# Four of the third batch's six head pairs transposed by DMA instead of by TensorE

## The chip, the cores and the metric

The kernel runs on one core of a Trainium2 chip. The metric is the device time of one execution in microseconds (us). The engines are called as in the profile: PE (TensorE matmul) and PEld (its weight load), DVE (VectorE), ACT (ScalarE), POOL (GpSimd) and SP (SyncE, which here only issues DMAs). Batches are counted from 0 as in the code: the "third batch" is batch 2.

## The reference

Attention with a squared ReLU in place of the softmax, followed by a gated feed-forward network whose gate is a ReLU. There are 8 batches, 12 heads, 448 positions and 64 elements per head; the network goes from 768 to 1536 and back to 768.

```python
scores = scale * np.matmul(q, k.transpose(0, 1, 3, 2))
attn = np.maximum(scores, 0.0) ** 2 / S
attn_out = np.matmul(attn, v)
x = attn_out.transpose(0, 2, 1, 3).reshape(B * S, H * D)
gate = np.maximum(x @ w_gate, 0.0)
val = x @ w_val
out = (gate * val) @ w_out
```

## The kernel before

The twelve heads of a batch are worked as six pairs, two pairs to a "quad". `k`, `q` and `v` of a batch are loaded by POOL's DMA queue in their natural layout and cast to bf16 on the way (`load_qk`, `load_v`, line 95), into two sets of buffers `kn`, `qn`, `vn` that alternate by batch. The scores need `k` and `q` with the head's 64 elements on the partitions, so both have to be transposed. There are two ways in the kernel:

- By PE, for batches 0 to 2 (`transposes`, lines 177 and 179): sixteen transposes of a pair go into one PSUM tile `kq_ps`, eight from `kn` and eight from `qn`, and one DVE copy brings them to `kq_sb`. `kq_ps` shares its three PSUM buffers with the score tiles `sc_ps`.
- By DMA, for batches 3 to 7 (`dma_transposes`, lines 151 and 154): DVE regroups `kn` into `kr` and `qn` into `qr`, one copy each for all twelve heads, and SP issues eight DMA transposes, four that write `kT` and four that write `qT`. `kr` and `qr` exist once, `kT` and `qT` twice (`NB` is 2). For batch b+1 this is done in the third of the eight steps of batch b.

The order of the work on every engine is the program's order: each instruction is pinned. `batch(b)` runs eight steps. A step n issues three tiles (`burst`: score tiles, or the begun product of a quad with `v`), squares the first two, and fills two gaps with units of the feed-forward network of batch b-1 (`gap`, `gv_unit`, `out_unit`). Work in `midway` is run in the middle of the next such unit; the PE transposes are put there by this table:

```python
PAIRS_AT = {0: [2], 1: [3], 3: [4], 4: [5], 7: [6, 7]}
```

Pairs 6 and 7 stand for pairs 0 and 1 of the next batch. `operands` returns the transposed tiles of a pair, and where `b >= PE_B` it only points at `kT` and `qT` and issues nothing. So batch 2's pairs 0 and 1 are transposed at the end of batch 1, its pairs 2 and 3 in steps 0 and 1 of batch 2, and its pairs 4 and 5 in steps 3 and 4. The first score tile of pair 2 is the last of the three tiles of step 2.

In the last step (n is 7) the product with `v` of the third quad is finished by `values()`, whose DVE cast (line 458) writes `xT`. SP also issues the stores of the output tiles `o_sb` (line 302), two for each tile of 128 rows, from three buffers. An output tile is scaled by ACT (line 294) before.

`load_qk(b + 1)` and `load_v(b + 1)` stand in step 0 of batch b, but POOL does little else and runs ahead in its queue until the buffer that a load writes is free.

Of the kernel before, what the change touches and what calls it, by code (L numbers as in the profile page):

```python
# [16 lines left out]
def kernel(  # L17
# [15 lines left out]
    nc = tc.nc  # L33

    B, H, S, D = q.shape
    d_model, d_ff = moe_w_gate.shape
# [3 lines left out]
    HP = H // 2  # L40
# [19 lines left out]
    def pin(ins):  # L60
        return tc.keep_in_program_order(ins)
# [53 lines left out]
    def load_qk(b, h0=0, h1=H):  # L115
        load_nat(kn_b[b % NB], k, b, h0, h1)
        load_nat(qn_b[b % NB], q, b, h0, h1)

    def load_v(b):
        load_nat(v_b[b % NB], v, b, 0, H)  # L120

    def low_values(b):

        t = v_b[b % NB].rearrange("p (q s h) i d -> p q s h i d", s=2, h=2)
        pin(nc.vector.tensor_copy(t[64:128, :, 1, :, 3, :], t[0:64, :, 1, :, 3, :]))
# [14 lines left out]
            dma_in(wo_sb[c], rows.rearrange("(kf p) m -> p kf m", p=128))  # L140


    PE_B = 3
    kT_b = [const.tile([128, HP, 512], BF16, name=f"kT{i}") for i in range(NB)]
    qT_b = [const.tile([128, HP, 512], BF16, name=f"qT{i}") for i in range(NB)]
    def dma_transposes(b):

        n = b % NB
        for nat, grp, tr in ((kn_b[n], kr, kT_b[n]), (qn_b[n], qr, qT_b[n])):
            o = grp.rearrange("p i (h d) -> p i h d", d=D)  # L150
            pin(nc.vector.tensor_copy(o, nat.rearrange("p h i d -> p i h d")))
            for i in range(4):
                r = 128 if i < 3 else 64
                pin(nc.sync.dma_start_transpose(out=tr[:, :, i * 128:i * 128 + r], in_=grp[0:r, i, :]))


    def operands(b, hp, bank=None):

        if b >= PE_B:
            n = b % NB  # L160
            return kT_b[n][:, hp, 0:S], qT_b[n][:, hp, 0:S]
        kq = transposes(b, hp, bank)
        return kq[:, 0:S], kq[:, 512:512 + S]
# [4 lines left out]
    def transposes(b, hp, bank):  # L168
        if bank is None:
            ps = psum.tile([128, 2048], BF16, name="kq_ps", tag="sc", bufs=3)  # L170
        else:
            ps = bank.bitcast(BF16)
        for t, c0 in ((kn_b[b % NB], 0), (qn_b[b % NB], 512)):
            for i in range(4):
                for h2 in range(2):
                    o = ps[h2 * 64:h2 * 64 + 64, c0 + i * 128:c0 + i * 128 + 128]
                    pin(nc.tensor.transpose(o, t[:, 2 * hp + h2, i, :], ident))  # L177
        kq = kqpool.tile([128, 512 + S], BF16, name="kq_sb")
        pin(nc.vector.tensor_copy(kq, ps[:, 0:512 + S]))
        return kq  # L180
# [9 lines left out]
    def relu2(src, dst, n):  # L190
        square_part(dst, relu_part(src, n))
# [25 lines left out]
    def av_rest(b, qd, attn, banks):  # L217
        for c in range(2):
            for i in range(3):
                for h2, o in HALVES:  # L220
                    mm(banks[c][o, :], v_b[b % NB][:, 4 * qd + 2 * c + h2, i, :], attn[:, 8 * c + 2 * i + h2, :], False, i == 2)
# [100 lines left out]
    def start_gaps(of):  # L322
        share[:] = [len(ffn), of, 0]

    def gap():

        n, of, i = share
        for _ in range((i + 1) * n // of - i * n // of):
            ffn.pop(0)()
        flush()  # L330
        share[2] = i + 1
# [22 lines left out]
    def transpose_pair(b, hp, bank=None):  # L354
        kqs[b, hp] = operands(b, hp, bank)

    def attn_of(b, qd):
        if (b, qd) not in attns:
            attns[b, qd] = atpool.tile([128, 14, S], BF16, name="attn")
        return attns[b, qd]  # L360

    def burst(b, tiles):

        todo, begun = [], None
        for qd, kind, c, i in tiles:
            attn = attn_of(b, qd)
            if kind == "pair":
                todo.append(scores(kqs[b, 2 * qd + c], i, attn, 8 * c + 2 * i))
            elif kind == "last":
                todo.append(scores_last((kqs[b, 2 * qd], kqs[b, 2 * qd + 1]), attn))  # L370
            else:
                ps = sc_tile()
                banks = [ps[:, c, :S] for c in range(2)]
                av_last(b, qd, attn, banks)
                begun = (qd, banks, ps[:, :, :S])
        return todo, begun
# [59 lines left out]
    def batch(b):  # L436

        gaps = [(1, 1)] * 8
        if b == 1:
            gaps = [(0, 1), (0, 1), (0, 1), (0, 1), (0, 1), (0, 1), (1, 1), (1, 1)]  # L440
        elif b == 2:
            gaps[5] = (0, 2)
        start_gaps(sum(map(sum, gaps)))
        for n in range(len(tiles_later) // 3):
            todo, begun = burst(b, tiles_later[3 * n:3 * n + 3])
            relu2(*todo[0])
            relu2(*todo[1])
            late.extend(todo[2:])
            if n == 1:
                low_values(b)  # L450
            if n == 0 and b < B - 1:
                load_qk(b + 1)
                load_v(b + 1)

            def values():
                qd, banks, both = begun
                av_rest(b, qd, attn_of(b, qd), banks)
                pin(nc.vector.tensor_copy(xT_of[b][:, 2 * qd:2 * qd + 2, :], both))  # L458

            for _ in range(gaps[n][0]):  # L460
                gap()
            for hp in PAIRS_AT.get(n, ()):
                if hp < HP:
                    midway.append(lambda hp=hp: transpose_pair(b, hp))
                elif b + 1 < B:
                    midway.append(lambda hp=hp: transpose_pair(b + 1, hp - HP))
            if begun and (b, n) == (1, 2):
                midway.append(values)
            elif begun:
                values()  # L470
            if b + 1 < B and n == 2 and b + 1 >= PE_B:
                dma_transposes(b + 1)
            for _ in range(gaps[n][1]):
                gap()

    for b in range(B):
        xT_of[b] = xpool.tile([128, KD, S], BF16, name="xT")
        if b == 0:
            first_batch()
        else:  # L480
            batch(b)
        if b + 1 < B:
            ffn.extend(ffn_units(b))
            if b == 0:
                for _ in range(7):
                    ffn.pop(0)()
                for hp in range(2):
                    midway.append(lambda hp=hp: transpose_pair(1, hp))
                ffn.pop(0)()
# [34 lines left out]
```

## Time and profile before

| | |
|---|---|
| median of 3 runs | 435.25 us (434.73 to 435.25) |
| the profiled execution | 435.1 us, of which the profile's span is 433.3 us |
| granted TensorE clock | 1.00 |
| PE / PEld busy | 98% / 58% of the span |
| DVE / ACT / POOL busy | 49% / 50% / 11% of the span |
| PE transposes of batches 1 and 2 | 192, each row 219 ns |
| `kq_sb` copies on DVE from `kq_ps` | 12, mean 654 ns |
| regrouping copies on DVE | 10, mean 950 and 953 ns |
| DMA transposes | 40, median 2.5 to 2.6 us from issue to landing |

The timeline of an engine shows for each piece its start, its length, the operation with its tiles, how many instructions are merged in it, and in brackets the idle time before it with what ended it. PE matmuls are pipelined: the length of a row holds the drain of the last one, so the pace is read from the starts of rows that follow each other.

### The profile page before, as it was taken

The numbers are of one execution on the slowest core, as the hardware profiler recorded it, in microseconds if no ns is written. First come the engines' busy times: TensorE is split into PE (matmuls) and PEld (weight loads), VectorE is DVE, ScalarE is ACT, GpSimd is POOL, SyncE is SP. The second block draws the span as 40 slices with busy tenths as digits, with TensorE's granted clock in tenths as the row PEclk, the third lists the DMA queues.
The fourth block names the chain that finished last, engine by engine and source line by source line (L and its number), as shares of the span: only waits on it lengthen the run. The fifth ranks groups of instructions, "written<-read, shape, count | busy, mean of one in ns | idle before, by whom it ended". The sixth has DMA issues, their size and how long they took to land.

```text
span 433.3 us, 11436 instructions
## 1 busy us (share of the span) xinstructions
PE 425.4 (98%) x5068; PEld 250.3 (58%) x5068; DVE 210.7 (49%) x334; ACT 218.0 (50%) x325; POOL 49.0 (11%) x71
## 2 busy tenths in 40 slices
PE   8899999999999999999999999999999999999996
PEld 4457655655565555655566555655566555566564
DVE  5952784556623655356532565435643454422210
ACT  4942666454554564465454645554545645532221
POOL 8424311100204000300004000010000000000001
PEclk9999999999999999999999999999999999999999
DMA  9999999905679770591517932170414100030014
GB/s 151 181 205 195 203 205 211 204 5 81 106 145 166 103 112 19 104 198 34 97 38 128 176 66 65 38 138 2 101 29 106 42 2 2 12 100 2 2 38 109
DMA packets 78513, 42.45 MB, mean 98 GB/s; under 512 B 48352, under 2 KB 74976, under 8 KB 78464
## 3 DMA queue, kind: packets, MB, share of 16 engines
q0 software_dynamic: 45120, 23.47, 40.6%
q1 hardware_dynamic: 32992, 18.01, 17.8%
q8 instruction: 39, 0.64, 0.6%
q10 hardware_dynamic: 352, 0.25, 0.2%
q14 instruction: 10, 0.08, 0.1%
HBM read 47.19 MB, written 11.01 MB: 134 GB/s over the span
## 4 chain that ended last, share of the span: by engine, by line
PE 84%; DMA 12%; POOL 2%; issue 1%; POOLq 0%; ACT 0%
PE o_ps L64 25%; PE g_ps L64 23%; PE v_ps L64 22%; PE sc_ps L64 13%; DMA qn<-in_q_dram 5%; DMA wo<-in_moe_w_out_dram 5%; DMA vn<-in_v_dram 2%; POOL qn L95 1%; PE kq_ps L177 1%; POOL kn L95 1%; POOL vn L95 0%; POOL out_dram L302 0%; POOLq L519 0%; ACT o_sb L294 0%; POOL ident L91 0%
## 5 line engine op out<-in xcount | busy, mean ns | idle before, releaser
L184 ACT ACTIVATE r_sb<-sc_ps 128x896 bf16<-128x896 f32 x168 | 145.1, 927 | 39.4 <-PE sc_ps L64 39.4
L188 DVE TENSOR_TENSOR attn<-r_sb 128x896 bf16<-128x896 bf16 x168 | 103.7, 623 | 92.2 <-ACT r_sb L184 92.1
L64 PE MATMUL g_ps<-xT,wg 128*64 128x448 bf16 x1152 | 126.1, 354 | 0.0
L64 PE MATMUL v_ps<-xT,wv 128*64 128x448 bf16 x1152 | 125.2, 352 | 0.0
L64 PE MATMUL o_ps<-wo,hT 128*64 128x384 bf16 (+1 forms) x1368 | 115.3, 324 | 0.3 <-DMA wo<-in_moe_w_out_dram 0.3
L271 DVE TENSOR_TENSOR hT<-v_ps,g_sb 128x448 bf16<-128x448 f32 x96 | 59.9, 624 | 88.4 <-PE v_ps L64 87.5
L64 PEld LDWEIGHTS <-hT 128*64 128x64 bf16 x1368 | 75.5, 110 | 37.8 <-issue 6.5
L265 ACT ACTIVATE g_sb<-g_ps 128x448 bf16<-128x448 f32 x96 | 52.3, 545 | 88.9 <-PE g_ps L64 88.9
L64 PEld LDWEIGHTS <-wg 128*64 128x64 bf16 x1152 | 63.4, 110 | 49.8 <-issue 13.1
L64 PEld LDWEIGHTS <-wv 128*64 128x64 bf16 x1152 | 66.2, 110 | 41.0
L294 ACT ACTIVATE o_sb<-o_ps 128x384 f32<-128x384 f32 (+1 forms) x57 | 27.9, 489 | 81.4 <-PE o_ps L64 81.4
L64 PE MATMUL sc_ps<-attn,vn 128*64 128x448 bf16 (+1 forms) x336 | 35.1, 354 | 0.0
L95 POOL DMA_DIRECT2D vn<-in_v_dram x16 | 12.1, 768 | 168.5 <-PE sc_ps L64 161.0
L458 DVE CAST xT<-sc_ps 128x896 bf16<-128x896 f32 x21 | 22.9, 1091 | 14.3 <-PE sc_ps L64 14.3
L64 PEld LDWEIGHTS <-vn 128*64 128x64 bf16 (+1 forms) x384 | 18.8, 109 | 16.5 <-issue 5.6
L64 PE MATMUL sc_ps<-qT,kT 64*64 64x448 bf16 x420 | 28.4, 357 | 0.0
L64 PE MATMUL sc_ps<-kq_sb 64*64 64x448 bf16 x252 | 19.0, 360 | 1.9 <-ACT r_sb L184 1.7
L95 POOL DMA_DIRECT2D kn<-in_k_dram x18 | 13.3, 762 | 46.8 <-PE kq_ps L177 45.2
L64 PEld LDWEIGHTS <-kT 64*64 64x64 bf16 x420 | 9.6, 105 | 14.3 <-issue 11.7
L302 POOL DMA_DIRECT2D out_dram<-o_sb x2 | 1.1, 558 | 146.2 <-ACT o_sb L294 146.2
L95 POOL DMA_DIRECT2D qn<-in_q_dram x20 | 14.6, 752 | 9.4 <-DMA vn<-in_v_dram 6.3
L64 PEld LDWEIGHTS <-kq_sb 64*64 64x64 bf16 x252 | 6.5, 105 | 13.3 <-issue 9.9
(32 smaller groups left out, 84.2 us busy)
## 6 DMA issues: line engine op xcount, KB each, us to landing
out_dram<-o_sb SPq DMA_DIRECT2D x54, 192.0 KB, 2.7
vn<-in_v_dram POOLq DMA_DIRECT2D x8, 384.0 KB, 7.7
kn<-in_k_dram POOLq DMA_DIRECT2D x7, 384.0 KB, 9.7
qn<-in_q_dram POOLq DMA_DIRECT2D x7, 384.0 KB, 12.2
vn<-in_v_dram POOLq DMA_DIRECT2D x8, 288.0 KB, 8.7
wo<-in_moe_w_out_dram POOLq DMA_DIRECT2D x2, 1152.0 KB, 20.0
kn<-in_k_dram POOLq DMA_DIRECT2D x7, 288.0 KB, 10.9
qn<-in_q_dram POOLq DMA_DIRECT2D x7, 288.0 KB, 13.0
```

Of the source, the lines that this page charges most:

```text
L64: pin(nc.tensor.matmul(o, lhsT=l, rhs=r, start=start, stop=stop, skip_group_check=True))
L95: pin(nc.gpsimd.dma_start(out=o, in_=i))
L177: pin(nc.tensor.transpose(o, t[:, 2 * hp + h2, i, :], ident))
L184: pin(nc.scalar.activation(r, src, AF.Relu))
L188: pin(nc.vector.tensor_tensor(dst, r, r, ALU.mult))
L265: pin(nc.scalar.activation(g_sb, g_ps, AF.Relu))
L271: pin(nc.vector.tensor_tensor(hT[:, mf, col:col + S], v_ps, g_sb, ALU.mult))
L294: pin(nc.scalar.activation(out=o_sb[:, c0:c1], in_=o_ps, func=AF.Copy, scale=float(out_scale)))
L302: pin(e.dma_start(out=segment_rows(b0, 2 * t + s)[:, m], in_=o_sb[s * 64:s * 64 + 64, m]))
L458: pin(nc.vector.tensor_copy(xT_of[b][:, 2 * qd:2 * qd + 2, :], both))
```

## The change

The test of which way a pair is transposed now depends on the pair too. Pairs 2 to 5 of batch 2 (heads 4 to 11) come by DMA; pairs 0 and 1 stay with PE. `dma_transposes` gets a first head `h0`, and is called for batch 2 with `h0 = 4` in the last step of batch 1, behind the cast of `values()` and ahead of the step's second gap. Its two DVE copies and its eight DMA transposes then cover eight heads of twelve. On SP they stand between the second and the third pair of output stores of batch 1. The rest of the kernel is as it was.

```diff
     PE_B = 3
+
+    def by_dma(b, hp):
+        return b >= PE_B or b == PE_B - 1 and hp >= 2
+
     kT_b = [const.tile([128, HP, 512], BF16, name=f"kT{i}") for i in range(NB)]
     qT_b = [const.tile([128, HP, 512], BF16, name=f"qT{i}") for i in range(NB)]
-    def dma_transposes(b):
+    def dma_transposes(b, h0=0):
 
         n = b % NB
         for nat, grp, tr in ((kn_b[n], kr, kT_b[n]), (qn_b[n], qr, qT_b[n])):
             o = grp.rearrange("p i (h d) -> p i h d", d=D)
-            pin(nc.vector.tensor_copy(o, nat.rearrange("p h i d -> p i h d")))
+            pin(nc.vector.tensor_copy(o[:, :, h0:H, :], nat[:, h0:H].rearrange("p h i d -> p i h d")))
             for i in range(4):
                 r = 128 if i < 3 else 64
-                pin(nc.sync.dma_start_transpose(out=tr[:, :, i * 128:i * 128 + r], in_=grp[0:r, i, :]))
+                pin(nc.sync.dma_start_transpose(out=tr[:, h0 // 2:HP, i * 128:i * 128 + r],
+                                                in_=grp[0:r, i, h0 * D:d_model]))
 
     def operands(b, hp, bank=None):
 
-        if b >= PE_B:
+        if by_dma(b, hp):
...
             if b + 1 < B and n == 2 and b + 1 >= PE_B:
                 dma_transposes(b + 1)
+            if n == 7 and b + 2 == PE_B:
+                dma_transposes(b + 1, 4)
             for _ in range(gaps[n][1]):
                 gap()
```

## The prediction

> **What bounds the kernel now.** I read the busy shares first, then the slices, then the stretches of whole batches, and last the timelines of PE, DVE, SP and POOL around 78 to 94 us, where the change acts. From the page:
>
> ```profile
> PE 425.4 (98%) x5068; PEld 250.3 (58%) x5068; DVE 210.7 (49%) x334; ACT 218.0 (50%) x325; POOL 49.0 (11%) x71
> DMA  9999999905679770591517932170414100030014
> ```
>
> PE is busy from end to end, so what leaves PE shortens the run and any wait of PE lengthens it. A slice is 10.8 us: the DMA engines are full through the first eight slices, to 87 us. The change puts its DMA transposes at 79 us, inside that stretch. PE's timeline where the transposes of pair (2,2), batch 2 and pair 2, stand, and where that pair is first used:
>
> ```profile
> 83.03 1.30 PE L64 MATMUL g_ps<-xT,wg 128*64 128x448 bf16 x12
> 84.17 0.39 PE L177 MATMUL kq_ps<-ident,kn 128*64 128x128 bf16 x8
> 84.39 0.39 PE L177 MATMUL kq_ps<-ident,qn 128*64 128x128 bf16 x8
> 84.61 1.30 PE L64 MATMUL v_ps<-xT,wv 128*64 128x448 bf16 x12
> ...
> 94.13 0.36 PE L64 MATMUL sc_ps<-attn,vn 64*64 64x448 bf16 x4
> 94.31 0.36 PE L64 MATMUL sc_ps<-kq_sb 64*64 64x448 bf16 x4
> ```
>
> Sixteen transposes take from 84.17 to 84.61, 0.44 us. The last row is the first score tile of pair (2,2): its operands are wanted at about 94.2. The same in the large, by stretches between the first gate matmuls of batches 2, 3, 4 and 5:
>
> ```profile
> 80.74:135.34 54.60, 54.60 (x682) 32.52 (x680) 28.00 (x43) 27.42 (x42) 7.27 (x10) 1.00 0.60 100
> ...
> 184.18:236.93 52.75, 52.75 (x615) 30.64 (x616) 25.46 (x39) 27.36 (x42) 4.49 (x7) 1.00 0.58 97
> ```
>
> Batch 4 has the feed-forward units of batch 2 but no PE transposes, and is 1.85 us shorter.
>
> **What is taken off.** Four pairs of 16 transposes: 4 x 0.44 = 1.77 us of PE, within 0.1 of the 1.85 above. Two pairs (0.88) lie ahead of the 94.2 point and two behind it. Four DVE copies of 0.66 us and four turns of a PSUM buffer go too; DVE is half idle in this batch, so I count them at nothing.
>
> **What is put on DVE.** At the end of batch 1:
>
> ```profile
> 77.31 1.09 DVE L458 CAST xT<-sc_ps 128x896 bf16<-128x896 f32 x1 [1.13 <-PE sc_ps L64]
> 78.73 1.22 DVE L179 COPY kq_sb<-kq_ps 128x960 bf16<-128x960 bf16 x2 [0.33 <-PE kq_ps L177]
> ```
>
> The regrouping copies come between these rows. Copies of 3072 elements take 0.95 us (950 and 953 ns), so 2048 take 0.63 in proportion: `kr` from 78.40 to 79.03, `qr` to 79.67, then the two `kq_sb` copies to 80.33 and 80.98. PE starts batch 2's first tile at 80.04 in the trace of before. It needs the first `kq_sb`, and its third tile the PSUM buffer that the second copy frees, at about 80.5 in the trace of before. So PE waits about 0.5 us here; 0.2 if the copies overlap at their ends as neighbours on DVE do, 0.8 if the gap of 0.36 us before the next gate matmuls comes on top. The PE transposes of (2,0) and (2,1), 78.1 to 79.0, do not wait.
>
> **What is put on SP.** The transposes start at 79.0, when `kr` is written; the four stores ahead of them are issued by 75. Issues of the full size, in batch 2 and without other traffic:
>
> ```profile
> 100.23 6.15 SPq L154 DMA_TRANSPOSE kT<-kr  x4
> 106.47 5.21 SPq L154 DMA_TRANSPOSE qT<-qr  x4
> ```
>
> The issue of one is 1.21 to 1.30 us, the half-height fourth one no shorter, so I take no gain from four blocks instead of six. In each of the five sets of the trace, one or two land late and hold up an issue for about 0.9 us. First issue to last landing is 12.7 us here. At that pace the last would land at 91.7, ahead of PE's need. That need is 94.2 - 0.88 + 0.5, about 93.8 after the change. The two stores behind them wait on SP from 80.7 to about 93, and the first reuse of their buffer is behind 114 us, so they cost nothing.
>
> **The traffic.** POOL's queue:
>
> ```profile
> 77.57 1.49 POOL L95 DMA_DIRECT2D vn<-in_v_dram  x2 [8.93 <-PE sc_ps L64]
> 113.69 1.49 POOL L95 DMA_DIRECT2D kn<-in_k_dram  x2 [34.63 <-PE kq_ps L177]
> ```
>
> The second row is batch 4's `kn` load, which waits for the last PE transpose of batch 2. That wait goes: the buffer is free when the regrouping copies and the transposes of (2,1) are done, near 79.1 (`kn`) and 79.7 (`qn`). So 1536 packets each of batch 4's `kn` and `qn` queue up behind batch 3's `vn`. The loads, which end near 86.5 before, then run on to about 94 by themselves. The transposes meet loads over their whole length, and no row shows that. The nearest rows are the output stores that SP issues into these loads, 69 to 82 us (first line), against all stores of the page (second), and the two queues in four short windows:
>
> ```profile
> DMA to landing us min/median/max: 5.2/5.8/6.5
> ```
> ```profile
> out_dram<-o_sb SPq DMA_DIRECT2D x54, 192.0 KB, 2.7
> ```
> ```profile
> q0 software_dynamic: 418, 0.19, 147.7%
> ```
> ```profile
> q1 hardware_dynamic: 109, 0.29, 79.8%
> q0 software_dynamic: 117, 0.05, 37.3%
> ```
> ```profile
> q1 hardware_dynamic: 549, 0.14, 122.6%
> ```
>
> The last three fences are loads alone (76 to 77 us), stores with loads (78 to 79) and transposes alone (204 to 204.5). Stores land 3.1 us later under load, and once their packets are in, the two queues share nearly packet for packet (109 to 117). Loads alone take 16 us / 418, 38 ns a packet on each of 16 engines, transposes 16 x 0.5 / 549, 14.6 ns. Alternating, a pair takes 53 ns. The eight DMAs have 3584 packets of one row of 256 bytes, 224 an engine, of which the first brings 32. So: first landing 79.0 + 5.8 = 84.8 (the stores' median; the transposes' own 2.5 plus 3.1 gives 84.6), then 192 x 53 ns = 10.2 us, then 0.9 us for the late one that every set has: 95.9.
>
> The ends: with the transposes at their own issue pace and only the delay of 3.1 added, 91.7 + 3.1 = 94.8; with no delay, 91.7. If loads are served first, the transposes end with the loads, and the engines are never idle: 7.5 us of loads left from before, 2 x 96 packets x 38 ns = 7.4, and 3.3 of transposes, from 79.0 to about 97.2, or 99 with the landing and the late one. I take 95.9, because the stores are nearest: same queue, same loads.
>
> [...]
>
> **The sum.** PE resumes at 95.9 where it was at 94.2: +1.7 us (the 0.88 saved ahead and the 0.5 lost on DVE are swallowed by the wait, which is 95.9 - 93.8 = 2.1 us). Behind it pairs 4 and 5 still save 0.88. Net +0.8. The profiled execution's 435.1 (its span of 433.3 and 1.8 around it) becomes 435.9; the median of before stands 0.15 above that execution, so 436.1. By terms: 435.25 - 1.77 + 0.5 + 2.1. Without any wait for the transposes it would be 434.0. Batch 3's regrouping, at about 100, finds `kr` free, and its transposes, though beside loads, have until 134.6.
>
> **The rivals.** (1) The transposes land by 93.8 and PE saves its 1.77 less 0.5: 433.6 (with 0.2 on DVE) to 434.3, faster. For it: 91.7 without load, and a store's bytes under load move as fast as alone once begun. Against it: 2.1 us are to spare at the pace without load, and the stores' later landing alone takes 3.1. Its point is a last landing before 94.2, 0.4 us late at most. (2) They land about a microsecond late, as with the end of 94.8: 434.4 to 436.1, no difference. (3) The loads go first and the last lands near 99: PE waits 5 us, 434.0 + 5.2 = 439.2. A wait that long may have a second price. At the start PE's first 18 matmuls on `blank` come every 187 ns to 4.5 us, later ones every 94: a slow phase after idling costs 18 x 93 ns = 1.7 us, which gives 440.9. [...] (4) That the work is not moved at all: excluded, since the program has 64 PE transposes fewer, and its score matmuls of pair 2 wait for the DMA transposes.
>
> **Chances.** Forecast (the last landing between 95.5 and 98): 0.45. Rival 1: 0.31. Rival 2: 0.12. Rival 3: 0.12. A measurement of this kernel tells about 0.2% from no change, 0.87 us. Faster, below 434.4, is rival 1: 0.31. Slower, above 436.1, is rival 3 and the part of the forecast that lands later than 95.9, 0.32 of the 0.45, since most unknowns (an engine that lags, a second late landing) push it that way: 0.44. No difference is rival 2 and the rest of the forecast, 0.13: 0.25. The range runs from rival 1's low end, 433.6, to rival 3's without the slow phase, 439.5.
>
> **What would show it.** In the profile after: no L177 rows beyond 79 us; batch 4's `kn` load near 79; landings of the first `kT` and `qT` near 5 to 6 us instead of 2.5; and on PE's row of `sc_ps<-qT,kT` near 94 an idle of about 2 us put down to a DMA. Wrong are the sharing if that idle is missing, the delay if the landings stay at 2.5, the DVE term if the start of batch 2 does not move by about half a microsecond.

## The result, and the profile after

The changed kernel takes 441.73 us (median of 4 runs, 440.87 to 442.07) against 434.99 us for the kernel before (4 runs on the same chip, 434.64 to 435.25): a ratio of 1.0153, with a 95% interval of 1.0141 to 1.0165. It is slower by 6.7 us. The profiled execution of the changed kernel took 440.87 us, its span 439.1.

The page of the changed kernel, part 1 and three rows of the slices (now 11.0 us each):

```profile
PE 425.5 (97%) x5004; PEld 248.9 (57%) x5004; DVE 209.4 (48%) x332; ACT 218.5 (50%) x325; POOL 49.4 (11%) x71
...
PE   8899999959999999999999999999999999999996
...
PEclk9999999988999999999999999999999999999999
DMA  9999999991617933294614935170412200030014
```

PE has 64 instructions fewer, yet the same busy time, and one slice, the ninth (88 to 99 us), is half empty. The granted clock dips there and in the next. The stretch from the first gate matmul of batch 2 to that of batch 3 in the changed kernel (span, then PE busy), counted from the end of the score tile ahead of each:

```profile
81.12:141.14 60.02, 54.76 (x614) 31.30 (x616) 25.36 (x39) 27.43 (x42) 5.79 (x9) 0.94 0.69 102
```

Counted the same way, 80.81 to 135.34, it was 54.53 before; the prediction's 54.60 starts 0.07 us earlier. All of the difference is in the timeline of PE of the changed kernel:

```profile
80.17 0.94 PE L64 MATMUL sc_ps<-kq_sb 64*64 64x448 bf16 x12 [0.36 <-DVE kq_sb L185]
81.05 1.33 PE L64 MATMUL g_ps<-xT,wg 128*64 128x448 bf16 x12
...
93.54 0.36 PE L64 MATMUL sc_ps<-attn,vn 64*64 64x448 bf16 x4
99.16 0.59 PE L64 MATMUL sc_ps<-qT,kT 64*64 64x448 bf16 x4 [5.26 <-DMA out_dram<-o_sb]
99.68 2.45 PE L64 MATMUL g_ps<-xT,wg 128*64 128x448 bf16 x12
101.92 1.85 PE L64 MATMUL v_ps<-xT,wv 128*64 128x448 bf16 x12
103.60 1.30 PE L64 MATMUL sc_ps<-attn,vn 128*64 128x448 bf16 x12
```

PE waits 5.26 us for the first score tile of pair (2,2). The name behind the arrow is that of a store, since a later store counts on the same semaphore as the first `kT` transpose (in the trace's landings the transpose is complete there at 87.4, the store not before 99.6, behind PE's start at 99.16); what lands at that moment is the last `qT` transpose (90.7 + 8.3 = 99.0). After the wait the next 24 gate and value matmuls take 3.92 us from start to start instead of 2.30 (94.60 to 96.90 before): PE runs at half pace until 103. The windows of the changed kernel show it (the column ahead of the last two is the granted clock):

```profile
93.00:96.00 3.00, 0.90 (x14) 0.14 (x8) 1.25 (x2) 0.92 (x1) 0.00 (x0) 1.00 1.38 181
96.00:99.00 3.00, 0.00 (x0) 0.00 (x0) 0.00 (x0) 0.00 (x0) 0.00 (x0) 0.53 1.24 231
99.00:103.00 4.00, 3.84 (x22) 1.82 (x24) 0.62 (x1) 1.46 (x2) 0.00 (x0) 0.50 0.08 23
103.00:107.00 4.00, 4.00 (x44) 2.25 (x40) 2.68 (x4) 0.54 (x1) 0.00 (x0) 1.00 0.00 0
```

The sum, against the profiled execution of before: the stretch 60.02 - 54.53 = 5.49, which is -1.77 for the transposes, 5.43 of waiting and 1.85 of half pace (1.62 in the 24 matmuls, 0.23 in the score tile), 5.51 together. The wait is 5.43 here and 5.26 in the row: without it the tile would start at 93.73, while the tile ahead of it still drains to 93.90. Ahead of the stretch stand 0.62, where PE waits for `kq_sb`, and 0.31 less because this execution was that much earlier already at 77.8 us. That is 5.80 in all, where the two spans differ by 439.1 - 433.3 = 5.8.

The DMA side, in the changed kernel: SP's timeline, then POOL's, then the landings of `kT` and of `qT` (two answers), and the two queues from 87.25 to 97.25 us (q0 is POOL's queue, q1 is SP's):

```profile
78.73 5.40 SPq L159 DMA_TRANSPOSE kT<-kr  x4
84.23 7.77 SPq L159 DMA_TRANSPOSE qT<-qr  x4
```
```profile
77.27 1.80 POOL L95 DMA_DIRECT2D vn<-in_v_dram  x2 [10.72 <-PE sc_ps L64]
79.64 1.49 POOL L95 DMA_DIRECT2D kn<-in_k_dram  x2 [0.57 <-issue]
81.11 1.52 POOL L95 DMA_DIRECT2D qn<-in_q_dram  x2
```
```profile
DMA to landing us min/median/max: 8.7/9.2/9.6
```
```profile
DMA to landing us min/median/max: 8.3/10.0/10.7
```
```profile
q0 software_dynamic: 2659, 1.16, 87.9%
q1 hardware_dynamic: 2691, 0.65, 50.6%
```

Batch 4's `kn` and `qn` go out at 79.6 and 81.1 instead of 113.7 and 115.2. The transposes, about 2.5 us each where they are alone, take 8.3 to 10.7, and loads and transposes move in equal numbers in these 10 us, 2659 packets to 2691. Ahead of that, from 79.5 to 82.5 us, only loads move, though SP issued its first transpose at 78.7; q1 has no packet there at all:

```profile
q0 software_dynamic: 1142, 0.52, 139.0%
```

### The profile page after: what moved, and what is told of

It is laid out like the page before. It is cut to its first block, busy times and chain, and to the rows that moved or that the text cites. A ratio compares the mean times of both kernels' runs of the same rounds, so it can differ in the third digit from the quotient of the medians.

```text
span 439.1 us, 11326 instructions
## 1 busy us (share of the span) xinstructions
PE 425.5 (97%) x5004; PEld 248.9 (57%) x5004; DVE 209.4 (48%) x332; ACT 218.5 (50%) x325; POOL 49.4 (11%) x71
## 4 chain that ended last, share of the span: by engine, by line
PE 87%; DMA 5%; DVE 2%; SPq 2%; ACT 1%; issue 1%; POOL 0%; POOLq 0%; DVEq 0%; ACTq 0%
PE g_ps L64 25%; PE v_ps L64 24%; PE o_ps L64 23%; PE sc_ps L64 14%; DMA qn<-in_q_dram 3%; SPq L159 2%; DMA out_dram<-o_sb 2%; ACT r_sb L190 1%; DMA kr<-in_k_dram 1%; DVE attn L194 1%; PE xT_ps L64 1%; PE kq_ps L183 1%; PE xT_ps L183 1%; DVE kq_sb L185 0%; POOL kn L95 0%
## 5 line engine op out<-in xcount | busy, mean ns | idle before, releaser
L194 DVE TENSOR_TENSOR attn<-r_sb 128x896 bf16<-128x896 bf16 x168 | 103.7, 623 | 96.3 <-ACT r_sb L190 96.2
L64 PE MATMUL sc_ps<-qT,kT 64*64 64x448 bf16 x476 | 32.3, 359 | 5.3 <-DMA out_dram<-o_sb 5.3
L64 PEld LDWEIGHTS <-kT 64*64 64x64 bf16 x476 | 10.9, 105 | 21.5 <-issue 13.1
L64 PE MATMUL sc_ps<-kq_sb 64*64 64x448 bf16 x196 | 15.4, 362 | 2.2 <-ACT r_sb L190 1.7
L64 PEld LDWEIGHTS <-kq_sb 64*64 64x64 bf16 x196 | 5.3, 104 | 12.2 <-issue 8.8
## 6 DMA issues: line engine op xcount, KB each, us to landing
kn<-in_k_dram POOLq DMA_DIRECT2D x7, 288.0 KB, 12.7
```

The costliest lines, as they stand in the source:

```text
L64: pin(nc.tensor.matmul(o, lhsT=l, rhs=r, start=start, stop=stop, skip_group_check=True))
L194: pin(nc.vector.tensor_tensor(dst, r, r, ALU.mult))
```

## The experiments

Theory S: the transposes share the DMA engines with the loads packet by packet, that sets their landing, and PE waits for it. Against it stood T (the DMA route is slow by itself), L (only batch 4's early loads matter) and A (any load in the way is enough). Ratios are to runs of the kernel before on the same chip: 434.79 us for the runs below whose names begin with `e1`, `e2`, `e4` and `e5`, and 434.97 us for `e3`, `e6` and `e7`.

**The gain alone** (`e1_gain_alone`), on the kernel before:

```diff
         if b >= PE_B:
...
+        if b == PE_B - 1 and hp >= 2:
+            return kqs[b, hp % 2]
         kq = transposes(b, hp, bank)
```

> The kernel before, in which pairs 2 to 5 of batch 2 use the transposed tiles of pairs 0 and 1, so their 64 PE transposes and four DVE copies are left out and nothing takes their place. All theories agree if the term was right: 435.0 - 1.77 = 433.2 us. If the PE transposes hide more (waits for PSUM buffers) it is below 432.9; if they were covered, near 435.

433.05 us, ratio 0.9962 (0.9949 to 0.9976): 1.7 us faster, the expected 1.77. The term for the 64 transposes was right. Batch 4's loads go out at 79.3 us in this kernel too: without transposes beside them they cost nothing that can be seen.

**DMA transposes done but not used** (`e2_dma_unused`), on the changed kernel:

```diff
     def by_dma(b, hp):
-        return b >= PE_B or b == PE_B - 1 and hp >= 2
+        return b >= PE_B
```

> The changed kernel, in which PE still transposes all six pairs and the DMA transposes are done but not used. DVE's two copies and the DMA traffic stay, PE's wait and the earlier loads of batch 4 go (they wait for PE again). Theory S (the transposes share the DMA engines with the loads packet by packet, and the landing sets PE): last qT landing near 92.5 us, since only batch 3's loads are in the way; time 435.0 plus about 0.6 for DVE's copies, 435.6. Rival T (the DMA route is slow by itself, through its issues and the pause in the engines, whatever the loads do): the same time, but the last landing again at 97 or later.

435.57 us, ratio 1.0016 (1.0007 to 1.0025): 0.8 us slower, 0.6 expected. The landings of `qT` in this kernel, and PE's start of batch 2:

```profile
DMA to landing us min/median/max: 3.8/5.6/6.8
```
```profile
80.63 0.94 PE L64 MATMUL sc_ps<-kq_sb 64*64 64x448 bf16 x12 [0.36 <-DVE kq_sb L185]
```

The last transpose was issued at 90.2 and landed at 94.0, where 92.5 was expected by S and 97 or later by T. The PE wait ahead of batch 2 is there, put down to DVE's `kq_sb`: the price of the two copies stands by itself. T is weakened, not yet excluded; S missed this landing by 1.5 us.

**Batch 3's v and batch 4's k and q held back** (`e4_loads_held`), on the changed kernel. POOL copies two elements out of the last-written part of `qT`, so its queue stands still until they are there:

```diff
+    held = const.tile([1, 2], BF16, name="held")
+    def hold_loads():
+        pin(nc.gpsimd.tensor_copy(held, qT_b[0][0:1, HP - 1, S - 2:S]))
...
                 load_qk(b + 1)
+                if b == 2:
+                    hold_loads()
                 load_v(b + 1)
```

> The changed kernel, with a two-element POOL copy out of qT placed ahead of the load of batch 3's v, so that this load and batch 4's k and q wait until the last DMA transpose of batch 2 has landed. Theory S: the transposes meet only the rest of batch 3's k and q loads, to about 82 us, and then run at their issue pace; last landing 90 to 92, no wait of PE, no slow clock: 435.0 - 1.77 + 0.6 = 433.8. Rival T: last landing at 97 or later, PE waits 3 us or more, 437 or above. Rival L (only batch 4's early loads matter): the same as S here, told apart in a later run that holds only those.

433.59 us, ratio 0.9967 (0.9955 to 0.998). In this kernel POOL waits in front of the load, the landings of `qT` are those of transposes alone, and PE passes pair (2,2) without a wait:

```profile
90.80 0.17 POOL L165 COPY held<-qT 1x2 bf16<-1x2 bf16 x1 [24.02 <-DMA qT<-qr]
91.32 1.50 POOL L95 DMA_DIRECT2D vn<-in_v_dram  x2 [0.34 <-PE v_ps L64]
```
```profile
DMA to landing us min/median/max: 2.3/2.4/2.4
```
```profile
93.54 0.36 PE L64 MATMUL sc_ps<-attn,vn 64*64 64x448 bf16 x4
93.73 0.36 PE L64 MATMUL sc_ps<-qT,kT 64*64 64x448 bf16 x4
```

T is excluded: same copies, same transposes, same order, and 8.1 us less than the changed kernel. Which of the loads does it, this run can't tell.

**Only batch 4's k and q held back** (`e3_batch4_held`): the same, with `if b == 3: hold_loads()` ahead of `load_qk(b + 1)`.

> The changed kernel, with the same two-element POOL copy placed one load later: batch 3's v goes out as before, and only batch 4's k and q wait for the last DMA transpose of batch 2. Rival L (batch 4's early loads are the trouble): the last qT lands about 94, where PE needs it (as in the run with unused DMA transposes, 94.0), PE waits 0 to 0.5 us, no half clock, 433.6 to 434.2. Rival A (any load in the way is enough, batch 3's v alone makes it late): landing near 97, PE waits 3 us, 436.5 to 437.

433.81 us, ratio 0.997 (0.9959 to 0.9981). The landings of `qT`:

```profile
DMA to landing us min/median/max: 2.3/3.5/5.6
```
```profile
93.95 0.36 PE L64 MATMUL sc_ps<-qT,kT 64*64 64x448 bf16 x4
```

Batch 3's `v` goes out at 77.5 beside the transposes and slows the first of them: the first `kT` lands at 87.4, as late as in the changed kernel. But `v` is used up before the last ones; the last lands at 91.4 (94 was expected), and PE goes on at 93.95 without a wait. L holds, A falls. What the change costs comes from two loads that its own freed buffers let go 34 us earlier.

**Three pairs instead of four** (`e6_three_pairs`): `hp >= 3` in `by_dma`, and `dma_transposes(b + 1, 6)`.

> The changed kernel with three pairs by DMA (3, 4 and 5) instead of four; loads as in the changed kernel. Pair 3 is wanted first near 100 us, pair 2 stays with PE. Theory S: 168 packets an engine at 60 ns from 82.4, a pause of 1.5, tail 0.6: last landing near 94.6, no PE wait. 435.0 - 1.33 + 0.4 for DVE's shorter copies = 434.1. Rival T (a late landing whatever the size, 97 to 100): up to 1 us of wait, 434.1 to 435.

433.99 us, ratio 0.9976 (0.9966 to 0.9986), 434.1 expected. Batch 4's `kn` load now waits for the PE transposes of pair 2 and goes out at 85.5, and the need is almost 7 us later. The last `qT` lands at 88.8 + 6.6 = 95.4, where pair 3 is wanted at 100.6. So the loss is no property of the DMA route, but of when the need falls.

**PE kept busy through the wait** (`e5_pe_kept_busy`), on the changed kernel, 25 calls of two matmuls on zeros into the score tile, which the scores then overwrite:

```diff
         ps = sc_tile()
+        idle_matmuls(ps[:, 0, :], idle)
...
+                                   25 if (b, qd, c, i) == (2, 1, 0, 0) else 0))
```

> The changed kernel with 50 matmuls on a tile of zeros ahead of the first score tile of pair 2 of batch 2, 4.7 us of PE work that lies inside its wait of 5.3 us. If the wait of PE itself causes the half clock seen after it, the clock stays at 1.00 and the time falls by the 1.9 us that the half-clock stretch costs, to about 439.8 against 441.7 of the changed kernel. Rival: the half clock has another cause, and the time stays near 441.7 or rises. The landing of the transposes stays near 99 us under both.

440.19 us, ratio 1.0133 (1.0108 to 1.0157); the changed kernel has 1.0153 (1.0141 to 1.0165). By times alone this does not decide, since the intervals overlap. The timeline does, and so does the clock during the rest of the wait and behind it:

```profile
94.44 4.92 PE L64 MATMUL sc_ps<-blank 128*64 128x448 bf16 x50
100.51 0.38 PE L64 MATMUL sc_ps<-qT,kT 64*64 64x448 bf16 x4 [1.15 <-DMA out_dram<-o_sb]
100.82 1.33 PE L64 MATMUL g_ps<-xT,wg 128*64 128x448 bf16 x12
101.98 1.30 PE L64 MATMUL v_ps<-xT,wv 128*64 128x448 bf16 x12
```
```profile
99.00:100.00 1.00, 0.36 (x4) 0.00 (x0) 0.00 (x0) 0.00 (x0) 0.00 (x0) 1.00 1.17 260
100.00:104.00 4.00, 3.49 (x38) 2.10 (x40) 1.23 (x2) 1.46 (x2) 0.00 (x0) 1.00 0.13 49
```

The clock stays at 1.00 and the gate matmuls keep their 1.16 us, so it is PE's wait that halves the clock. This holds for the profiled execution, 440.39 us. The longest of the four, 442.54 us, has a mean clock of 0.995 where the others have 0.998 to 1.000, so its clock probably fell all the same; it has no trace. The transposes landed 0.7 us later in this run, counted from the same point of the program, which eats part of the 1.9 us.

**Loads held, and the regrouping copies behind the `kq_sb` copies** (`e7_held_and_copies_later`), the loads as in the first run with held loads:

```diff
             if n == 7 and b + 2 == PE_B:
-                dma_transposes(b + 1, 4)
+                midway.append(lambda: dma_transposes(b + 1, 4))
```

> The run with held loads, in which DVE's two regrouping copies stand behind the two kq_sb copies instead of ahead of them. If those copies are what PE waits for at the start of batch 2, the 0.6 us there go: 433.6 - 0.6 = 433.0, the time of the gain alone. The transposes start 1.2 us later, last landing near 92, ahead of the need near 93. If the transposes are late by that, the wait comes back and the time is 433.6 or more.

433.19 us, ratio 0.996 (0.9947 to 0.9974), the time of the gain alone. DVE's order in this kernel, and PE's start of batch 2:

```profile
78.62 1.22 DVE L189 COPY kq_sb<-kq_ps 128x960 bf16<-128x960 bf16 x2 [0.33 <-PE kq_ps L187]
79.76 0.68 DVE L156 COPY kr<-kn 128x2048 bf16<-128x2048 bf16 x1
80.36 0.69 DVE L156 COPY qr<-qn 128x2048 bf16<-128x2048 bf16 x1
```
```profile
79.93 0.76 PE L64 MATMUL sc_ps<-kq_sb 64*64 64x448 bf16 x12
```

No idle stands at the start of batch 2 any more, and the last transposes still land at 92.0, ahead of 93.3. This version beats the kernel before by 1.8 us; its interval and that of the run with only the loads held overlap.

## Why the prediction was wrong, step by step

The path was right: batch 4's loads go out early, the transposes share with them, and PE waits for the last landing. The step that failed is the size of that landing, forecast at 95.9 (95.6 in the time of this execution) and measured at 99.0, and with it the half clock behind the longer wait, which the forecast's sum left out.

- **The saved PE transposes: right.** 1.77 forecast; 1.7 measured by the gain alone.
- **DVE's copies: right.** 0.5 forecast (0.2 to 0.8); 0.62 in the changed kernel, 0.36 with `v` held too, none where the copies come later.
- **The need of pair 2: right within 0.2.** 93.8 forecast, 93.5 in the time of the changed kernel, which runs 0.3 earlier; 93.73 there by the start that the tile would have had.
- **Batch 4's loads going out near 79: right**, at 79.6 and 81.1, and they are the cause.
- **First landing: the term that failed most.** 84.8 forecast, 84.5 in the time of this execution; 87.4 measured (78.73 + 8.7). I took the stores' 5.8 us. The late start in it was right: the first packets of the transposes move after 82.6, 4.0 us behind their issue, as do those of a store issued at 69.2 in the trace of before (1.13 us there for the stores issued at 130.2, 174.4, 222.3 and 275.9, with nothing else moving). What follows was too short: a store brings four packets to an engine, and a transpose 32, which come to 1.9 us at the 59.8 ns that a load and a transpose packet took together. The last 2.6 us to the landing are not settled. The engines stood still for about 1 us in this stretch (28 packets from 86 to 87), but in the run with PE kept busy they did not, and its first landing took 8.6 us too. By itself this term would have cost nothing: with batch 4's loads held the first landing is at 87.4 as well, and PE does not wait.
- **Sharing one to one: right for the counts, 2659 to 2691. Its price: too small.** A count over 10 us does not tell single packets in turn from longer turns of equal length. 53 ns for a pair of packets forecast, as the sum of both alone; 16 x 10 / 2675 = 59.8 ns measured. From first to last landing that made 11.6 us for 10.2. That is the price while batch 4's loads last; with the loads held and the copies later the transposes move 488 packets in the half microsecond from 87.0, with no load beside them, where the changed kernel moves 133 from 88.5 beside 129 of the loads. Together: +2.9, +1.4 and -0.9 for the pause counted apart put the last landing at 99.0 instead of 95.6, and the wait at 5.4 us (5.26 of them idle) instead of 2.1.
- **The half clock: given too little weight.** The sum of the forecast had no term for it; only rival 3 had one, an estimate from the slow matmuls at the start (18 x 93 ns). The half pace took 1.85 us where rival 3 had 1.7. Rival 3 with its slow phase came out at 440.9, the profiled execution at 440.87 and the median at 441.73; I gave it 0.12 and ended the range ahead of that phase. Its reason, loads first, was wrong: from 87.25 to 97.25 the loads moved 2659 packets and the transposes 2691, so the agreement of its time is luck. The mechanism of the forecast gave that time, once its terms had their size. A wait forecast at 2.1 us with unknown terms of 1 to 3 us was close to the point at which the clock fell here, 2.3 us behind the last matmul, so the two errors were not independent.
- **Smaller slips, which do not move the sum.** First issue to last landing of the set shown is 14.0 us, not 12.7 (the last transpose lands after 3.8 us, not 2.5; the other four sets have 12.5 to 12.9), so the end without load was 93.0 there. The last load of before lands at 88.4, not near 86.5, a reading that only rival 3 uses. The stretches differ by 1.78, not 1.85, which fits the 1.77 better.
- **When the clock fell, and when it did not.** Here it fell at 96.2, 2.3 us after the last matmul ended, and was full again 3.9 us after PE resumed. A wait of 1.15 us, with PE kept busy, left it at 1.00. The traces have no single limit: behind the last matmul of a run the clock falls after 2.2 us in the changed kernel (435.4 to 437.5), and in the trace of before it is still full after 3.7 us. The rows of the changed kernel (first two) and of the kernel before:

```profile
435.40:437.40 2.00, 0.00 (x0) 0.00 (x0) 0.00 (x0) 0.32 (x1) 0.72 (x2) 1.00 0.61 160
437.60:439.10 1.50, 0.00 (x0) 0.00 (x0) 0.00 (x0) 0.00 (x0) 0.00 (x0) 0.50 0.00 0
```
```profile
429.60:433.30 3.70, 0.00 (x0) 0.00 (x0) 0.00 (x0) 0.31 (x1) 0.72 (x2) 1.00 0.33 89
```

What stays open: the runs of the changed kernel differ by 1.2 us (440.87 to 442.07), and no trace shows which term varies. The last landing with `v` alone beside the transposes was 94.0 in one kernel and 91.4 in another.

## What to carry to other kernels

When work is moved off an engine, look at which buffers it frees earlier and which queue waits for them: POOL was waiting for the very instructions that were removed, and its loads then ran into the transfers that replaced them. A transfer that shares its engines is to be costed by its packets an engine and the measured pace of a pair of packets (here 224 and 59.8 ns), not by the landing of another transfer with an eighth of the packets (a store's 4 an engine against a transpose's 32). A long PE wait can cost more than itself: here 5.4 us of wait brought 1.85 us of half pace behind it. The shortest idle time at which the clock fell in these traces is 2.2 us, and the longest that left it full is 3.7, so a wait between the two may go either way.

## What was not expected of the hardware

- **The engines often stand still soon after a packet of an `instruction` queue that falls between transposes.** In the changed kernel the queues q0 and q1 move 13 and 15 packets from 86 to 87 us, against 111 and 105 from 85 to 85.5 us, a half microsecond that also has one packet of the `instruction` queue (q8):

```profile
q0 software_dynamic: 111, 0.05, 80.6%
q1 hardware_dynamic: 105, 0.03, 45.8%
q8 instruction: 1, 0.02, 15.3%
```

  In the trace of before, four of the five sets of transposes have such a packet (at 101.4, 154.0, 210.4 and 309.5) within about 1 us ahead of a pause of 1 to 2 us; the fifth has two packets of another instruction queue (q14, at 255.0 and 257.0) and a milder pause. In the run with the later copies no such packet falls between 80.5 and 92 us (one stands at 80.4, as the first transpose is issued), and all eight transposes land after 2.4 us. It does not always follow: in the run with PE kept busy a q8 packet falls at 85.2, and from 86 to 87 the queues still move 220 and 181 packets. The two were only seen together; the packet was not tested as a cause.
- **A regrouping copy and POOL's issue of a load are both slower side by side.** The `qr` copy takes 0.94 us in the changed kernel, beside POOL's `vn` issue of 1.80 us, and 0.68 with the loads held; that `vn` issue takes 1.50 there. The same pair, 0.94 and 1.80, stands in the runs with unused transposes and with batch 4 held. It explains 0.26 of the 0.62 us ahead of batch 2. Lines of the changed kernel and of the run with held loads:

```profile
78.61 0.94 DVE L156 COPY qr<-qn 128x2048 bf16<-128x2048 bf16 x1
```
```profile
78.86 0.68 DVE L156 COPY qr<-qn 128x2048 bf16<-128x2048 bf16 x1
```
